# Attention with a leaky-ReLU network: chunk 3's x turned by the DMA crossbar, and product steps placed anew

## The chip, the core and the metric

The kernel runs on one core of a Trainium2 chip. A core has five engines with instruction streams of their own: TensorE (PE, matrix products into PSUM; its weight loads are listed as PEld), VectorE (DVE), ScalarE (ACT), GpSimd (POOL) and SyncE (SP). They meet only at semaphores. Here POOL's and SP's main work is to issue DMA transfers: POOL those that also convert fp32 to bf16, SP the others, among them the DMA transposes ("crossbar"). The metric is the device time of one execution in microseconds.

## What is computed

Attention over 4 batches, 8 heads, 768 positions and 64 values a head, and behind it a two-layer network on the result:

```python
scores = scale * np.matmul(q, k.transpose(0, 1, 3, 2))
causal = rel >= 0
stream_keep = causal & (is_sink | in_win)      # 4 sink keys, window of 64
mask = np.where(retr[0, :, 0, 0, None, None], full_mask, stream_mask)
scores = np.where(mask[None, :, :, :], scores, -1000000000.0)
a = np.exp(scores - max) / sum
x = (a @ v).transpose(0, 2, 1, 3).reshape(3072, 512)
h = x @ w_in                                   # 512 -> 2048, "product 1"
out = np.maximum(0.01 * h, h) @ w_out          # 2048 -> 512, "product 2"
```

Heads 0, 2 and 6 are "retrieval" heads (all earlier keys), the other five are "stream" heads (sinks and window).

## The kernel before

The 3072 rows are cut into eight chunks of 384 (`CH`). `ORDER` (L57) gives each chunk its batch and half: chunks 2 and 3 are the second halves of batches 0 and 1, chunks 4 and 5 the first halves of batches 2 and 3, chunks 6 and 7 their second halves.

The order of work is written out by hand as lists of closures. `run` calls them in order; since each engine's stream is in order, this sets the order on every engine. There are three kinds:

- *Slots* of attention (`Attention.slots`, L413). A second-half chunk has 21 units: five for each retrieval head (groups of keys), one for each stream head, and one for the sinks. In slot t, unit t gets its scores (TensorE into a `psS` bank, L329 for retrieval, L364 for stream, L309 for sinks), the exponential on ACT (L334, L369, L312), and a mask on DVE where one is needed (L337, L339, L373). In the same slot the unit `lag` slots earlier is multiplied with the values (L298, into a `po` bank). After the last unit of a pair of heads, `finish` (L386) adds the sinks' part, and DVE divides by the sums (`linv` L395, `xs` L397). Then x must be turned, so that the features lie along the partitions: `x_t` (L400).
- *Ticks* of product 1 (`in_slots`, L557): four matmuls of 128x384 (L563) into a `ph` bank and a leaky ReLU on ACT into `g` (L565); 16 in a chunk. Each tick reads the turned x (`xt`) of all four pairs of heads.
- *Steps* of product 2 (`out_slots`, L582): 2 to 4 matmuls of 128x512 (L589) into a `py` bank; after 5, 5 and 6 steps a tile of 128 rows is complete, DVE copies it (L595) and SP sends it out (L596); 16 steps in a chunk.

Each tag of PSUM has two banks (`BANKS`, L54): `ph`, `psS`, `po`, `py`.

`x_t` has two ways. Without `cross`, three transposes on TensorE (L407) go into a PSUM bank, and ACT (L409) or DVE (L411) copies it into `xt`; this happens three slots after `finish`, so that such an attention has 21 + `lag` + 3 slots. With `cross`, SP issues one DMA transpose from `xs` to `xt` (L402) right after `finish`, and there are 21 + `lag` slots.

Chunks 0 and 1 are done at the start. Then L783 runs chunk 2's attention (`lag` 3, transposes on TensorE into `ph`, copies on ACT; 27 slots) merged with 14 steps of product 2: the last four of chunk 0 and the first ten of chunk 1. `merge` (L618) spreads one list evenly over another. After it come stages n = 2 to 7 (loop at L787). Stage n does the ticks of chunk n, the steps of chunk n-1 and the attention of chunk n+1. `turn_dma(n+2)` puts two crossbar transfers of keys and queries on SP, `v_shift` two copies of values, `load_qk` and `load_v` further loads on POOL, and `spreads(n+2)` are DVE copies that spread the turned keys into `kt`; they are laid into slots (`both`, `into`). In stage 2, chunk 3's attention turns x on TensorE into `psS` banks with copies on DVE (27 slots). From stage 3 on (`n > 2`), attentions use the crossbar, and the last nine places of the list (`rest`) come after the attention, to cover the transfer.

Before the change, L798 to L807 set this:

```python
a = Attention(n + 1, xt_eng="v", cross=n > 2).slots(lag=2 if n > 2 else 3)
a = into(a, extra) if n > 2 else a
ms = merge(in_slots(n), outs)
rest = ms[-9:] if a and n > 2 else []
```

Of the kernel before, what the change touches and what calls it, by code (L numbers as in the profile page):

```python
# [21 lines left out]
def kernel(  # L22
# [36 lines left out]
    def bank(tag, shape, dtype):  # L59
        return ps.tile(shape, dtype, name=tag, tag=tag, bufs=BANKS[tag])  # L60
# [46 lines left out]
    def load_qk(n, nms="kq"):  # L107
        b, c = ORDER[n]
        for nm in nms:
            t = rot.tile([128, 3, H, D], BF16, name=f"{nm}b", tag=f"{nm}b", bufs=1)  # L110
            raw[nm, n] = t
            for g in range(3):
                nc.gpsimd.dma_start(out=t[:, g], in_=nat[nm][b, c, :, :, g])  # L113

    def load_v(n, gs=range(3)):
        b, c = ORDER[n]
        for g in gs:
            nc.gpsimd.dma_start(out=va[b][:, 3 * c + g, :, 0:D], in_=nat["v"][b, c, :, :, g])  # L118
# [3 lines left out]
    def load_sinks(b, eng=None):  # L122
        vsf[b] = rot.tile([32, D], FP32, name="vsf", tag="vsf", bufs=2)
        (eng or nc.sync).dma_start(out=vsf[b][:], in_=v[b, :, 0:NS, :])

    def sink_values(b, eng):
        n = H - 1
        eng.tensor_tensor(
            vs[b % 2][0:32, 1:H, 0:D],
            vsf[b].rearrange("p (o d) -> p o d", o=1).to_broadcast([32, n, D]),  # L130
            m_sink[0:32, 1:H].rearrange("p (h o) -> p h o", o=1).to_broadcast([32, n, D]),
            op=ALU.mult)
# [8 lines left out]
    def v_shift(n, eng=None):  # L141
        eng = eng or nc.sync
        i, c = ORDER[n]
        lo, hi = (0, 2) if c == 0 else (2, 5)
        eng.dma_start(out=vb[i][0:64, lo:hi], in_=va[i][64:128, lo:hi])
        eng.dma_start(out=vb[i][64:128, lo:hi], in_=va[i][0:64, lo + 1 : hi + 1])
# [77 lines left out]
    def turn_dma(n):  # L224
        qx[n] = rot.tile([128, 3, 4, 128], BF16, name="qd", tag="qd", bufs=3)
        raw["kx", n] = rot.tile([128, 3, 4, 128], BF16, name="kd", tag="kd", bufs=2)
        for nm, dst in (("k", raw["kx", n]), ("q", qx[n])):
            nc.sync.dma_start_transpose(out=dst.rearrange("p g q t -> p (g q) t"),
                                        in_=raw[nm, n].rearrange("p g h d -> p (g h d)"))

    def spreads(n):
        b, c = ORDER[n]

        def spread(g, hh):
            r = slice(64 * hh, 64 * hh + 64)
            o = CH * c + 128 * g
            nc.vector.tensor_copy(kt[b % 2][hh][r, :, o : o + 128], raw["kx", n][r, g])  # L237

        r = [lambda g=g, hh=hh: spread(g, hh) for g in range(3) for hh in range(2)]
        if c == 0:  # L240
            r += sink_keys_by(b)
        return r
# [4 lines left out]
    def into(slots, extra):  # L247
        r, extra = [], list(extra)
        for j, s in enumerate(slots):
            r.append(s)  # L250
            if 5 * j >= 2 * len(slots) and extra:
                r.append(extra.pop(0))
                if len(extra) > len(slots) - j - 2:
                    r.append(extra.pop(0))
        return r + extra
# [301 lines left out]
    def in_slots(n, tags=("ph",)):  # L557
        def tick(t):
            if n not in gs:
                gs[n] = rot.tile([128, NG, CH], BF16, name="g", tag="g", bufs=2)  # L560
            ph = bank(tags[t % len(tags)], [128, 512], FP32)
            for g in range(KG):
                nc.tensor.matmul(ph[:, 0:CH], lhsT=w_in_bf[:, g, 128 * t : 128 * t + 128],  # L563
                                 rhs=xts[n][:, g, :] if n else xts[0][:, :, g, :], start=(g == 0), stop=(g == KG - 1))
            nc.scalar.activation(out=gs[n][:, t, :], in_=ph[:, 0:CH], func=ACTF.Prelu, alpha=0.01)  # L565

        return [lambda t=t: tick(t) for t in range(NG)]
# [14 lines left out]
    def out_slots(n, tags=("py", "py", "py"), halves=False):  # L582
        slots = []

        def part(tt, lo, hi, tag, c0, c1):
            if lo == 0:
                py[n] = bank(tag, [128, 512], FP32)
            for ng in range(lo, hi):
                nc.tensor.matmul(py[n][:, 0 : c1 - c0], lhsT=gs[n][:, ng, 128 * tt : 128 * tt + 128],  # L589
                                 rhs=w_out_bf[:, ng, c0:c1], start=(ng == 0), stop=(ng == NG - 1))  # L590
            if hi == NG:
                o = rot.tile([128, DM], FP32, name="o", tag="o", bufs=6)
                b, c = ORDER[n]
                r0 = S * b + CH * c + 128 * tt
                nc.vector.tensor_copy(o[:, 0 : c1 - c0], py[n][:, 0 : c1 - c0])  # L595
                nc.sync.dma_start(out=out[r0 : r0 + 128, c0:c1], in_=o[:, 0 : c1 - c0])  # L596

        for tt in range(3):
            if halves and tt == 2:
                slots.append(lambda: part(2, 0, NG, "py", 0, 256))  # L600
                slots.append(lambda: part(2, 0, NG, "psS", 256, 384))
                slots.append(lambda: part(2, 0, NG, "po", 384, 512))
                continue
            lo = 0
            for w in ([3, 3, 3, 3, 4], [3, 3, 3, 3, 4], [3, 3, 3, 3, 2, 2])[tt]:
                slots.append(lambda tt=tt, lo=lo, w=w: part(tt, lo, lo + w, tags[tt], 0, DM))
                lo += w
        return slots

    def run(*lists):  # L610
        for l in lists:
            for f in l:
                f()

    def both(s, e):
        return lambda: (s(), e and e())

    def merge(ms, as_):  # L618

        r, done = [], 0  # L620
        for j, m in enumerate(ms):
            want = (j + 1) * len(as_) // len(ms)
            r += as_[done:want] + [m]
            done = want
        return r + as_[done:]
# [152 lines left out]
    o0, o1 = out_slots(0), out_slots(1)  # L778
# [1 line left out]
    run(spreads(2))  # L780
    run(o0[6:12])
    v_shift(3)
    run(merge(o0[12:] + o1[0:10], Attention(2, xt_tag="ph").slots(lag=3)))  # L783
    run(spreads(3))
    outs = o1[10:]

    for n in range(2, NCH):  # L787
        a, extra = [], ()
        if n + 2 < NCH:
            turn_dma(n + 2)  # L790
            v_shift(n + 2)
            extra = spreads(n + 2)
            if ORDER[n + 2][1] == 0:
                load_sinks(ORDER[n + 2][0], nc.gpsimd)
                sink_values(ORDER[n + 2][0], nc.gpsimd)
            if n + 3 < NCH:
                load_qk(n + 3)
                load_v(n + 3)  # L798
        if n + 1 < NCH:
            a = Attention(n + 1, xt_eng="v", cross=n > 2).slots(lag=2 if n > 2 else 3)  # L800
            a = into(a, extra) if n > 2 else a
        ms = merge(in_slots(n), outs)
        rest = ms[-9:] if a and n > 2 else []
        if n == 2:
            a, rest = [both(s, e) for s, e in zip(a[:-3], [None] * 16 + extra)], [ms[-4], a[-3], ms[-3], a[-2], a[-1], ms[-2], ms[-1]]
            ms = ms[:-4] + rest
        run(merge(ms[: len(ms) - len(rest)], a), rest)  # L807
        outs = out_slots(n) if n + 1 < NCH else out_slots(n, ("psS", "psS", "py"), True)
    run(outs)
# [35 lines left out]
```

## Time and profile before

| | us |
|---|---|
| median of five runs | 235.76 |
| lowest and highest | 234.3, 236.02 |
| the profiled execution | 235.92 |
| its span in the profile | 234.1 |

The runs are 235.92, 236.02, 234.3, 235.76 and 234.76 us. The profile is of one execution; its span runs from the first to the last instruction, so that the execution's time is 1.8 us longer. The profile lists each instruction with line, engine, start and duration. "L563 PE MATMUL ph<-xt,w_in_bf 128x384 x4" reads: four matmuls of line 563, which read `xt` and `w_in_bf` and write 384 columns of a `ph` bank. "[0.24 <-DVE xs L397]" means that the engine stood idle for 0.24 us before and that DVE's instruction of L397 ended this. The next stage boundaries can be read from the first score of each attention: chunk 2's at 56.05 us, chunk 3's at 72.96, chunk 4's at 95.73, chunk 5's at 120.54.

The sixteen crossbar transfers of x that are there before (chunks 4 to 7) take 1.18 us of SP's time each in the median, and 2.3 to 7.7 us from issue to landing, 5.0 in the median.

### The profile page before, as it was taken

How to read it: one execution, taken by the hardware profiler on the slowest of the kernel's cores; microseconds unless marked ns; L12 is line 12 of the kernel's file. 1: busy time of each engine (PE TensorE's matmuls, PEld its weight loads, DVE VectorE, ACT ScalarE, POOL GpSimd, SP SyncE). 2: the span in 40 equal slices, each digit the busy share in tenths (PEclk: the TensorE clock that was granted, in tenths of full speed). 3: DMA queues.
4: the chain of work that ended last, by engine and by line, in shares of the span. 5: the costliest groups of instructions: out<-in, count | busy, mean ns of one | idle time of the engine just before them, and what ended most of it. 6: DMA issues, size and time to landing. Idle time of an engine off the chain costs nothing.

```text
span 234.1 us, 5117 instructions
## 1 busy us (share of the span) xinstructions
PE 225.6 (96%) x2080; PEld 139.5 (60%) x2080; DVE 98.4 (42%) x282; ACT 127.9 (55%) x275; POOL 71.3 (30%) x87
## 2 busy tenths in 40 slices
PE   7868999999999999999999999999999999999995
PEld 5657876645664676666556655666556665555554
DVE  7885568014566357357324451156212341111122
ACT  5757765722775785655355545765556763434300
POOL 8949534207419319439104800000000000000000
PEclk9999999999999999999999999999999999999999
DMA  9999999999999999999999992920210221111112
GB/s 132 152 166 180 194 207 167 179 117 160 157 143 262 180 167 127 172 171 153 135 144 186 175 138 80 215 64 18 81 45 0 64 59 40 45 45 45 43 50 91
DMA packets 109481, 28.98 MB, mean 124 GB/s; under 512 B 101249, under 2 KB 105745, under 8 KB 109457
## 3 DMA queue, kind: packets, MB, share of 16 engines
q0 software_dynamic: 77088, 13.39, 78.2%
q1 hardware_dynamic: 31312, 15.00, 32.2%
q10 hardware_dynamic: 1056, 0.26, 0.5%
q8 instruction: 16, 0.26, 0.5%
q14 instruction: 9, 0.07, 0.1%
HBM read 27.30 MB, written 6.29 MB: 143 GB/s over the span
## 4 chain that ended last, share of the span: by engine, by line
PE 87%; POOL 5%; DMA 4%; DVE 1%; ACT 0%; issue 0%; POOLq 0%
PE py L589 31%; PE ph L563 30%; PE po L298 7%; PE psS L329 5%; DMA w_in_bf<-in_moe_w_in_dram 4%; PE psS L589 3%; PE psS L364 3%; PE psS L563 2%; PE psS L309 2%; PE ph L576 1%; POOL kb L113 1%; POOL va L118 1%; POOL qb L113 1%; POOL k L104 1%; POOL q L105 1%; DVE xs L397 1%
## 5 line engine op out<-in xcount | busy, mean ns | idle before, releaser
L589 PE MATMUL py<-w_out_bf,g 128*128 128x512 bf16 (+1 forms) x352 | 90.9, 374 | 0.0
L563 PE MATMUL ph<-xt,w_in_bf 128*128 128x384 bf16 x448 | 90.3, 326 | 0.0
L565 ACT ACTIVATE g<-ph 128x384 bf16<-128x384 f32 x112 | 55.0, 491 | 57.4 <-PE ph L563 56.4
L563 PEld LDWEIGHTS <-w_in_bf 128*128 128x128 bf16 x480 | 44.1, 98 | 31.3
L589 PEld LDWEIGHTS <-g 128*128 128x128 bf16 x416 | 35.9, 98 | 25.8
L334 ACT ACTIVATE at<-psS 128x384 bf16<-128x384 f32 x78 | 36.9, 488 | 18.6 <-PE psS L329 18.4
L595 DVE COPY o<-py 128x512 f32<-128x512 f32 (+1 forms) x22 | 14.9, 678 | 50.7 <-PE py L589 50.3
L113 POOL DMA_DIRECT2D kb<-in_k_dram x21 | 18.7, 904 | 32.6 <-DMA kd<-kb 31.9
L329 PE MATMUL psS<-qd,kt 128*128 128x384 bf16 (+2 forms) x90 | 23.0, 294 | 0.4 <-ACT at L334 0.3
L118 POOL DMA_DIRECT2D va<-in_v_dram x24 | 21.4, 911 | 5.1 <-DMA w_in_bf<-in_moe_w_in_dram 3.3
L113 POOL DMA_DIRECT2D qb<-in_q_dram x21 | 18.7, 910 | 5.9 <-DMA w_in_bf<-in_moe_w_in_dram 1.8
L298 PE MATMUL po<-va,at 128*128 128x65 bf16 x228 | 19.2, 193 | 0.0
L369 ACT ACTIVATE ats<-psS 128x384 bf16<-128x384 f32 x35 | 16.7, 488 | 3.6 <-PE psS L364 3.1
L373 DVE TENSOR_TENSOR ats<-ats,m_win 128x384 bf16<-128x384 bf16 x35 | 12.4, 358 | 14.0 <-ACT ats L369 13.4
L298 PEld LDWEIGHTS <-at 128*128 128x128 bf16 x234 | 14.8, 98 | 4.8 <-issue 0.2
L397 DVE TENSOR_TENSOR xs<-po,linv 128x384 bf16<-128x384 f32 x27 | 15.0, 557 | 0.9
L237 DVE COPY kt<-kd 64x512 bf16<-64x512 bf16 x36 | 14.5, 403 | 1.5 <-DMA kd<-kb 1.0
L329 PEld LDWEIGHTS <-kt 128*128 128x128 bf16 x99 | 9.4, 97 | 8.0 <-issue 0.9
L364 PEld LDWEIGHTS <-kt 128*128 128x128 bf16 x210 | 10.6, 98 | 5.4
L339 DVE TENSOR_TENSOR at<-at,m_caus 128x128 bf16<-128x128 bf16 x21 | 4.7, 223 | 21.4 <-ACT at L334 21.3
L298 PEld LDWEIGHTS <-ats 128*128 128x128 bf16 x210 | 10.4, 97 | 4.0 <-DVE xs L397 0.4
L395 DVE RECIPROCAL linv<-po 128x6 f32<-128x6 f32 x27 | 5.2, 193 | 15.7 <-PE po L298 15.7
(143 smaller groups left out, 206.6 us busy)
## 6 DMA issues: line engine op xcount, KB each, us to landing
out_dram<-o SPq DMA_DIRECT2D x23, 256.0 KB, 3.2
va<-in_v_dram POOLq DMA_DIRECT2D x24, 128.0 KB, 7.6
kb<-in_k_dram POOLq DMA_DIRECT2D x21, 128.0 KB, 5.3
qb<-in_q_dram POOLq DMA_DIRECT2D x21, 128.0 KB, 7.0
w_in_bf<-in_moe_w_in_dram POOLq DMA_DIRECT2D x4, 512.0 KB, 10.1
w_out_bf<-in_moe_w_out_dram POOLq DMA_DIRECT2D x4, 512.0 KB, 13.4
vb<-va SPq DMA_DIRECT2D x8, 195.0 KB, 4.1
vb<-va SPq DMA_DIRECT2D x4, 130.0 KB, 3.4
```

Of the source, the lines that this page charges most:

```text
L113: nc.gpsimd.dma_start(out=t[:, g], in_=nat[nm][b, c, :, :, g])
L118: nc.gpsimd.dma_start(out=va[b][:, 3 * c + g, :, 0:D], in_=nat["v"][b, c, :, :, g])
L298: nc.tensor.matmul(o, lhsT=lhsT, rhs=rhs, start=first, stop=False, skip_group_check=True)
L329: nc.tensor.matmul(s[:, off : off + w], lhsT=kt[i][hh][:, p, 128 * kj : 128 * kj + 128], rhs=q_of(n, p, lo, CH), start=(j == 0), stop=(j = ...
L334: nc.scalar.activation(out=a[:, 0:off], in_=s[:, 0:off], func=ACTF.Exp, scale=SM)
L364: nc.tensor.matmul(s[:, 64 * m : 64 * m + 64], lhsT=kt[i][hh][:, p, k0 : k0 + 128], rhs=q_of(n, p, 64 * m, 64 * m + 64), start=(m == 0), s ...
L369: nc.scalar.activation(out=av_, in_=s[:, 0:CH].rearrange("p (j e f) -> p j e f", j=3, e=2), func=ACTF.Exp, scale=SM)
L397: nc.vector.tensor_tensor(xs[:], po[:, :, :, 0:D], linv.to_broadcast([128, 3, 2, D]), op=ALU.mult)
L563: nc.tensor.matmul(ph[:, 0:CH], lhsT=w_in_bf[:, g, 128 * t : 128 * t + 128], rhs=xts[n][:, g, :] if n else xts[0][:, :, g, :], start=(g == ...
L565: nc.scalar.activation(out=gs[n][:, t, :], in_=ph[:, 0:CH], func=ACTF.Prelu, alpha=0.01)
L589: nc.tensor.matmul(py[n][:, 0 : c1 - c0], lhsT=gs[n][:, ng, 128 * tt : 128 * tt + 128], rhs=w_out_bf[:, ng, c0:c1], start=(ng == 0), stop= ...
L595: nc.vector.tensor_copy(o[:, 0 : c1 - c0], py[n][:, 0 : c1 - c0])
```

## The change

Three edits. First, all attentions from chunk 3 on use the crossbar (`cross=True`); chunk 3's has 24 slots instead of 27. Second, stage 3 begins with the first eight steps of chunk 2's product 2 (`outs[:8]`); the other eight are merged with its 16 ticks. Third, a new function `tail` lays four places of a list among the first three slots of another and puts the other slots behind them; it is used for the end of chunk 2's attention and of chunk 3's. For chunk 2's, ten steps are merged with the first 12 slots and the last four go through `tail` with the other 15 slots.

```diff
+    def tail(ms, a):
+
+        return [a[0], ms[0], a[1], ms[1], a[2], ms[2], ms[3], *a[3:]]
...
-    run(merge(o0[12:] + o1[0:10], Attention(2, xt_tag="ph").slots(lag=3)))
+    a2, m2 = Attention(2, xt_tag="ph").slots(lag=3), o0[12:] + o1[0:10]
+    run(merge(m2[:10], a2[:12]), tail(m2[10:], a2[12:]))
...
-            a = Attention(n + 1, xt_eng="v", cross=n > 2).slots(lag=2 if n > 2 else 3)
+            a = Attention(n + 1, cross=True).slots(lag=2 if n > 2 else 3)
             a = into(a, extra) if n > 2 else a
-        ms = merge(in_slots(n), outs)
+        ms = outs[:8] + merge(in_slots(n), outs[8:]) if n == 3 else merge(in_slots(n), outs)
         rest = ms[-9:] if a and n > 2 else []
         if n == 2:
-            a, rest = [both(s, e) for s, e in zip(a[:-3], [None] * 16 + extra)], [ms[-4], a[-3], ms[-3], a[-2], a[-1], ms[-2], ms[-1]]
-            ms = ms[:-4] + rest
+            a = [both(s, e) for s, e in zip(a, [None] * 15 + extra + [None])]
+            rest = tail(ms[-6:-2], a[-3:]) + ms[-2:]
+            ms, a = ms[:-6] + rest, a[:-3]
```

Counted from the order of instructions that this gives: chunk 2's attention from slot 15 to slot 26 has no product step between its slots (before, steps stood among them to the end). In stage 2 the eight spreading copies move from slots 16 to 23 to slots 15 to 22. In the stages from 4 on TensorE's order is as before. On SP, the four transfers of chunk 3's x stand behind chunk 4's value shifts and ahead of an output transfer and chunk 5's transposes.

## The prediction

> **What bounds the kernel now.** I read the page first, then the waits, then windows by stage, then the timeline of the two places that the change touches. Busy times and the chain of the page:
>
> ```profile
> PE 225.6 (96%) x2080; PEld 139.5 (60%) x2080; DVE 98.4 (42%) x282; ACT 127.9 (55%) x275; POOL 71.3 (30%) x87
> ...
> PE 87%; POOL 5%; DMA 4%; DVE 1%; ACT 0%; issue 0%; POOLq 0%
> ```
>
> TensorE carries 87% of the chain that ended last. So only three things count here: matmuls removed, new time in which TensorE stands still, and old time in which it stands still. A busy row says little about the last two, since matmuls overlap (a 128x384 one shows 0.33 us, yet four start 0.65 us apart): I compare starts. The windows of the two touched stages and the following one, and below them four early microseconds:
>
> ```profile
> 56.05:72.96 16.91, 16.67 (x194) 10.41 (x193) 7.56 (x21) 11.12 (x25) 8.63 (x10) 1.00 1.91 178
> 72.96:95.73 22.77, 22.42 (x235) 14.42 (x234) 13.69 (x39) 16.43 (x37) 13.94 (x17) 1.00 1.77 167
> 95.73:120.54 24.81, 24.81 (x212) 14.73 (x211) 11.36 (x30) 12.82 (x29) 9.52 (x12) 1.00 1.62 155
> ...
> 16.00:20.00 4.00, 2.19 (x35) 2.01 (x36) 2.61 (x10) 1.70 (x4) 2.30 (x3) 1.00 2.00 177
> ```
>
> The columns are length, then busy time of PE, PEld, DVE, ACT and POOL, then the granted clock. The end of chunk 2's attention:
>
> ```profile
> 70.87 0.81 PE L589 MATMUL py<-w_out_bf,g 128*128 128x512 bf16 x3
> 71.08 0.20 DVE L395 RECIPROCAL linv<-po 128x6 f32<-128x6 f32 x1 [1.02 <-PE po L298]
> 71.31 0.56 DVE L397 TENSOR_TENSOR xs<-po,linv 128x384 bf16<-128x384 f32 x1
> 71.92 0.34 PE L407 MATMUL ph<-ident,xs 128*128 128x128 bf16 x3 [0.24 <-DVE xs L397]
> 72.30 0.49 ACT L409 ACTIVATE xt<-ph 128x384 bf16<-128x384 bf16 x1 [2.25 <-PE ph L407]
> ```
>
> The three product steps from 70.87 keep TensorE supplied until 71.52; the transposes start at 71.92. So 0.40 us is lost, although the chain from weighted values to transposed x takes 1.05 us: a step of 0.65 us covers the rest, and the step after the transposes (0.86 us) covers their copy on ACT. In chunk 3's attention:
>
> ```profile
> 88.36 0.33 PE L407 MATMUL psS<-ident,xs 128*128 128x128 bf16 x3
> 89.01 0.33 PE L329 MATMUL psS<-qd,kt 128*128 128x256 bf16 x2 [0.32 <-ACT at L334]
> ```
>
> Three transposes take 0.16 us, so the score could start at 88.52; it starts at 89.01, because the transposes hold one of two psS banks and the other is still read by an exponential. Start to start I find 0.49 us lost here, 0.08 before the transposes at 82.87, and 0.14 and 0.21 near 74.6 and 75.8, where scores wait for exponentials and for DVE's spreading of keys.
>
> **The change, part by part.** Times are us.
>
> Part 1, chunk 3's x by crossbar: twelve transposes go, 4 x 0.16 = -0.65 on TensorE. The four DVE copies (0.35 each) go too, and are worth nothing: DVE is busy 13.69 of 22.77. With the transposes go their two waits, -0.49 and -0.08. The stage's first slots get a product step between third and fourth score, and DVE spreads the keys of chunk 3 before, while TensorE waits in part 2; that takes away up to the other 0.35. Sum -1.57; lower end of the gain 0.65 (waits reappear elsewhere).
>
> Part 2, the tail of chunk 2's attention. This attention has 27 slots, not 18. The new order puts the last four product steps after slots 12, 13 and 14 (the last two together), so that slots 15 to 26 run with none between: six score units, six weightings, three sets of transposes. Their work on TensorE by the timeline's spacings: five scores at 0.16, one stream unit 0.17, weightings 1.45 (three of 0.27, one of 0.19, five of 0.09), transposes 3 x 0.16: 2.90; with the next score (0.16) and first tick of product 1 (0.65) 3.71. What it takes, counted from the end of the last product step: score to exponential 0.36 (72.96 to 73.33), start of an exponential to the score that reuses its bank 0.54 (88.47 to 89.01), ACT's pitch 0.385 (pairs listed at 0.87). Scores at 0.00, 0.43, 0.90, 1.34; exponentials at 0.36, 0.80, 1.26, 1.70. DVE first empties the product's bank (0.20 to 0.81), then linv and xs of the second pair end at 1.60; the fourth pair's weightings use that pair's po bank, so they start at 1.65 and the transposes at 1.74, the fifth score at 1.90, the sixth (bank) at 2.24. ACT copies x at 2.12, exponentials 2.51 and 2.89. The last mask follows 0.52 behind (69.18 to 69.70) and takes 0.36: weightings 3.82, linv 4.30 (0.48, as 70.60 to 71.08), xs 4.53, transposes 5.14, copy 5.52 to 6.01. The first tick's fourth matmul reads that copy: 6.06, over at 6.22. Lost 6.22 - 3.71 = 2.51, against 0.40: +2.11.
> Bounds. Below: only the covering step of 0.65 is missing, +0.65. Above: the score slots are serial, 0.36 + 0.54 = 0.90 each, the sixth exponential at 4.86 and not 2.89, end 8.19: 4.48 lost, +4.08. I take 2.11: ACT's and DVE's rows give it instruction by instruction.
>
> Part 3, the next stage begins with eight steps of product 2 (chunk 2's, ready): same matmuls, another order, 0. It covers the crossbar. From the last weightings of chunk 3 to its first tick stand five ticks (3.25), two product steps and a part (0.43), then eight (5.4) and five slots: about 10. Needed: 1.3 from weightings to issue (113.59 to 114.86 for chunk 4) and 2.3 to 7.7 to landing, the spread of the sixteen such transfers; chunk 5's first tick at 120.71 shows no wait 5.9 after issue. Queues: SP now issues four transposes of about 1.2 behind chunk 4's value shifts and ahead of the out transfer and chunk 5's key transposes. It stands idle from 87.6 to 95.4, so three lie there; the last adds about 1.2 ahead of an out transfer that waits for its copy anyway. POOL's loads of chunk 6 come behind chunk 5's transposes; no row of TensorE after 96 waits for a load. Price 0; if that cover is gone, the first tick of chunk 3 waits.
> ACT sees fewer evacuations while the eight steps run and denser ones later: a tick is 0.65 and its evacuation 0.49; old stage three had ACT busy 12.82 of 24.81. Price 0, bounds 0 and 0.5.
>
> The clock: the window 16 to 20 has TensorE busy 2.19 of 4.00, with one idle stretch of 1.26, at granted clock 1.00. My tail's longest idle stretch is 1.05 (4.09 to 5.14). I add nothing.
> The Trainium skill, "TensorE: Matmul & The Clock Gate", section "HAM oscillation", warns against idle gaps over about 3.4 us, after which the clock halves; were that to strike here, an estimate is one such window at half speed, +1.7, a sum of 238.0. The rule speaks against gathering idle time in a tail, but this gap stays under it.
>
> Sum: +2.11 - 1.57 = +0.54 on an execution of 235.92 (span 234.1 and 1.8 around it): 236.5. The median of the runs is 235.76, 0.16 lower, so the forecast for it is 236.3.
>
> **The rivals.** First, serial score slots: in the tail each score waits for the exponential just before, as at 89.01, because ACT is late with copies. Place: slots 15 to 20; price +4.08 - 1.57 = +2.5, 238.3, slower. For it: that row. Against: two psS banks alternate and ACT's pitch is 0.385. It decides from a tail of 6.9 (a loss of 2.75) upward.
> Second, the tail costs little: weightings fill the gaps and only the missing step shows, +0.65 - 1.57 = -0.9, 234.8. For it: the six score slots hold 2.3 of work against 2.7 of chain. Against: the finishing chain of 1.05 has nothing beside it.
> Third, the crossbar isn't in time: the last transfer has to share the queues with a pair of key and query transposes (up to 6.4 of issue), landing 15.4 after the weightings where 10 are covered: +5.4, 241.7 with the sum. Against: those stand behind it on SP.
>
> **How the numbers follow.** Forecast 0.54, serial slots 0.29, cheap tail 0.13, late crossbar 0.04. A measurement of this kernel can tell about 0.5%, 1.2 us. No change by that: 0.50 of the forecast's 0.54 and 0.06 of the cheap tail's 0.13. Slower: serial slots 0.29, late crossbar 0.04, 0.03 of the forecast. Faster: the cheap tail's other 0.07, where some gain that I don't see is added, and 0.01 of the forecast. Range: from the cheap tail, 234.9, to the serial slots, 238.3; outside lie the late crossbar, the worst of both bounds at once (+4.08 - 0.65, 239.2) and parts of both edges.
>
> **What would show it.** The stretch from chunk 2's first score to chunk 3's first: 16.91 now, 18.9 forecast (16.91 - 0.40 + 2.41). From there to chunk 4's first score: 22.77 becomes about 21.3. The tail's weightings should wait for DVE, one transpose row should show some 1.05 idle. No L407 or L411 rows after 80, four more transposes at L402. No wait for a DMA at the first tick of chunk 3. Wrong would be a tail over 6.9, a wait for xt at L563, a clock under 1.00, or waits in stage three.

## The result

The changed kernel takes 235.55 us in the median of 43 runs (234.56 to 237.97), the kernel before 234.81 in the median of 80 run beside it: a ratio of 1.004, 95% interval 1.0026 to 1.0054. It is slower by 0.4%, which is inside the half per cent that the prediction called no change (the interval ends just above it), and on the side where its sum lay (+0.54 us forecast; the ratio stands for +0.6 to +1.3 us). Here and below, a ratio leaves out executions that took over 1.5% more than the fastest of the same kernel.

The page of one changed execution (span 233.1 us, its time 234.84):

```profile
PE 224.2 (96%) x2068; PEld 138.7 (60%) x2068; DVE 98.2 (42%) x278; ACT 128.5 (55%) x275; POOL 71.2 (31%) x87
...
PE 88%; POOL 4%; DMA 3%; ACT 2%; DVE 2%; issue 0%; POOLq 0%
```

Twelve matmuls and four DVE copies are gone; TensorE still carries the chain. This span is a microsecond shorter than the one shown of before, which is no gain: chunk 1's sink scores, ahead of anything that the change touches, start at 25.56 us here and at 27.31 there, and over all profiles of this study that start lies between 25.1 and 28.0. So I compare stretches. The windows from chunk 2's first score to chunk 3's, on to chunk 4's and on to chunk 5's (columns as in the prediction):

```profile
54.30:73.08 18.78, 17.30 (x195) 10.64 (x194) 8.27 (x24) 10.94 (x24) 11.19 (x14) 1.00 1.69 210
73.08:94.41 21.33, 21.33 (x225) 13.76 (x223) 13.02 (x33) 16.72 (x38) 11.53 (x14) 1.00 2.01 157
94.41:119.22 24.81, 24.81 (x212) 14.73 (x211) 10.63 (x30) 13.31 (x29) 8.89 (x10) 1.00 1.40 151
```

The first stretch grew from 16.91 to 18.78 (+1.87), the second shrank from 22.77 to 21.33 (-1.44), the third is the same to the hundredth. Net +0.43. The tail of chunk 2's attention in the timeline, from its first bare score to the first tick of product 1, all engines, a selection:

```profile
67.70 0.33 PE L329 MATMUL psS<-qd,kt 128*128 128x384 bf16 x1
...
68.14 0.33 PE L329 MATMUL psS<-qd,kt 128*128 128x384 bf16 x1
...
68.61 0.32 PE L329 MATMUL psS<-qd,kt 128*128 128x384 bf16 x1
...
69.12 0.33 PE L329 MATMUL psS<-qd,kt 128*128 128x384 bf16 x1
...
70.02 0.34 PE L364 MATMUL psS<-qd,kt 128*128 128x64 bf16 x6
...
70.61 0.51 ACT L369 ACTIVATE ats<-psS 128x384 bf16<-128x384 f32 x1
70.77 0.29 DVE L337 TENSOR_TENSOR at<-at,m_caus 128x256 bf16<-128x256 bf16 x1 [0.53 <-ACT at L334]
...
71.12 0.27 PE L298 MATMUL po<-va,at 128*128 128x65 bf16 x3 [0.41 <-DVE at L337]
71.15 0.36 DVE L373 TENSOR_TENSOR ats<-ats,m_win 128x384 bf16<-128x384 bf16 x1
...
71.57 0.20 PE L298 MATMUL po<-vb,ats 128*128 128x65 bf16 x1 [0.18 <-DVE ats L373]
...
72.06 0.20 DVE L395 RECIPROCAL linv<-po 128x6 f32<-128x6 f32 x1 [0.55 <-PE po L298]
72.29 0.56 DVE L397 TENSOR_TENSOR xs<-po,linv 128x384 bf16<-128x384 f32 x1
...
72.90 0.34 PE L407 MATMUL ph<-ident,xs 128*128 128x128 bf16 x3 [0.88 <-DVE xs L397]
73.08 0.33 PE L329 MATMUL psS<-qd,kt 128*128 128x384 bf16 x1
...
73.24 0.90 PE L563 MATMUL ph<-xt,w_in_bf 128*128 128x384 bf16 x4
73.28 0.49 ACT L409 ACTIVATE xt<-ph 128x384 bf16<-128x384 bf16 x1 [1.77 <-PE ph L407]
```

Read it from the bracket at the end of the lines from 70.77 on: TensorE waits for a mask, for the next mask, then for the division, while nothing else is queued. The first tick's four matmuls take 0.90 instead of 0.81, since the fourth waits for the copy that ends at 73.77. In the second stretch, the place where a score used to wait for a psS bank now reads:

```profile
87.77 0.33 PE L329 MATMUL psS<-qd,kt 128*128 128x384 bf16 x1
87.93 0.25 PE L298 MATMUL po<-va,at 128*128 128x65 bf16 x3
88.02 0.81 PE L563 MATMUL ph<-xt,w_in_bf 128*128 128x384 bf16 x4
88.67 0.33 PE L329 MATMUL psS<-qd,kt 128*128 128x256 bf16 x2
```

Each starts when the one before has gone through (0.16, 0.09, 0.65): no transposes, no wait. The crossbar transfers are twenty now instead of sixteen, and nobody waits for them:

```profile
L402 SPq DMA_TRANSPOSE xt<-xs x20: 1179/1182/2252, 83.5 to 193.6; - x20
...
DMA to landing us min/median/max: 2.3/3.3/6.0
```

One thing doesn't show in this profile. In 11 of 44 executions of the changed kernel the mean granted clock is 0.991 to 0.993, else 0.998 to 1.000. Those 11 take 237.09 us in the mean, the other 33 take 235.36. I call such an execution one with a dip. Of another 80 executions of the kernel before, measured beside the experiments, 4 have a dip; the other 76 take 234.87 in the mean. So at full clock the change costs 235.36 - 234.87 = +0.49 us (standard error 0.14), as in the stretches; executions with a dip, a quarter of all and 1.7 us longer in the mean, add about 0.4 to the mean, where 4 of 80 add about 0.1 to that of the kernel before. Chance alone would seldom give 11 of 44 against 4 of 80 (0.003 by Fisher's exact test).

### The profile page after: what moved, and what is told of

It reads as the page before. It is cut to its first block, busy times and chain, and to the rows that moved or that the text cites. A ratio compares the mean times of both kernels' runs of the same rounds, so it can differ in the third digit from the quotient of the medians.

```text
span 233.1 us, 5099 instructions
## 1 busy us (share of the span) xinstructions
PE 224.2 (96%) x2068; PEld 138.7 (60%) x2068; DVE 98.2 (42%) x278; ACT 128.5 (55%) x275; POOL 71.2 (31%) x87
## 4 chain that ended last, share of the span: by engine, by line
PE 88%; POOL 4%; DMA 3%; ACT 2%; DVE 2%; issue 0%; POOLq 0%
PE py L589 32%; PE ph L563 30%; PE po L298 6%; PE psS L329 5%; PE psS L589 3%; DMA kb<-in_k_dram 3%; PE psS L364 3%; PE psS L563 2%; PE ph L576 2%; PE psS L309 2%; ACT at L334 1%; POOL va L118 1%; POOL k L104 1%; POOL q L105 1%; DVE xs L397 1%; POOL kb L113 1%
## 5 line engine op out<-in xcount | busy, mean ns | idle before, releaser
L329 PE MATMUL psS<-qd,kt 128*128 128x384 bf16 (+2 forms) x90 | 23.1, 294 | 0.0
L237 DVE COPY kt<-kd 64x512 bf16<-64x512 bf16 x36 | 15.1, 419 | 0.6
L339 DVE TENSOR_TENSOR at<-at,m_caus 128x128 bf16<-128x128 bf16 x21 | 5.4, 260 | 20.7 <-ACT at L334 20.6
```

The source lines that it names most:

```text
L329: nc.tensor.matmul(s[:, off : off + w], lhsT=kt[i][hh][:, p, 128 * kj : 128 * kj + 128], rhs=q_of(n, p, lo, CH), start=(j == 0), stop=(j = ...
```

## The experiments

Each run was compared with the kernel before on the same chip. "Stretch" is the time in one profile from chunk 2's first score to chunk 4's: 39.68 before, 40.11 after. "Dips" counts the executions with a mean clock of 0.993 or below.

**Even end: the crossbar and the new head of stage 3 without the tail.**

```diff
-    run(merge(m2[:10], a2[:12]), tail(m2[10:], a2[12:]))
+    run(merge(m2, a2))
```

> The changed kernel with chunk 2's attention merged evenly with its 14 product steps again, as before the change; the crossbar for chunk 3 and the eight product steps at the head of stage 3 stay. If the sum of the prediction holds (tail +2.1, crossbar and freed banks -1.57), this is 1.57 us faster than the kernel before: 0.9933 of it; the stretch from chunk 2's first score to chunk 3's is 16.9 and from there to chunk 4's 21.3. If the loss of the change lies in the crossbar part or the new head of stage 3 instead, it is no faster than before. If dips of the granted clock come from the tail, its runs show 0.991 to 0.993 about as seldom as the kernel before.

Measured: ratio 0.9986 (0.996 to 1.0013); stretch 16.91 + 21.35 = 38.26, so -1.42, close to the forecast -1.57; no dip in 12 executions. The stretch confirms the second part of the sum. The ratio does not show all of it.

**The tail alone, on the kernel before.**

```diff
-    run(merge(o0[12:] + o1[0:10], Attention(2, xt_tag="ph").slots(lag=3)))
+    a2, m2 = Attention(2, xt_tag="ph").slots(lag=3), o0[12:] + o1[0:10]
+    run(merge(m2[:10], a2[:12]), tail(m2[10:], a2[12:]))
```

> The kernel before with the new end of chunk 2's attention alone. By the sum: +2.1 us in executions at full clock, 1.009 of before, with the first stretch at 19.0 and the second at 22.4 to 22.8. If the clock's dips come from this tail, about a quarter of its runs show a mean granted clock of 0.991 to 0.993 and are 1.5 to 2 us longer still. If the tail is cheap (rival two): +0.65, 1.003.

Measured: ratio 1.0072 (1.0044 to 1.01), +1.7 us (+1.5 at full clock, in the mean of nine); stretch 18.78 + 22.65 = 41.43, +1.75; 2 dips in 11. The profile also has a wait of 0.47 us for the queries ahead of chunk 2's first score, outside the stretch. The two parts add up: +1.75 - 1.42 = +0.33 against +0.43 for the whole change. The cheap tail (+0.65) is excluded.

**No cover: crossbar for chunk 3, even end, but stage 3 begins as before.**

```diff
-        ms = outs[:8] + merge(in_slots(n), outs[8:]) if n == 3 else merge(in_slots(n), outs)
+        ms = merge(in_slots(n), outs)
```

> As the first, but stage 3 begins with ticks and steps in turn, as before the change: crossbar for chunk 3 with nothing put ahead to cover it. From the last weightings of chunk 3 some 3.2 us of work stand before its first tick, where the last transfer needs 1.3 to its issue and 2.3 to 7.7 to land. If the eight steps are what covers it: TensorE waits 0.4 to 5.8 at the first tick, some 3 in the middle, so the kernel is about 3 us slower than the first of these. If the transfer is quick enough anyway, the two are equal.

Measured: ratio 1.0142 (1.0104 to 1.0179), median 238.75; 4 dips in 6. The two executions at full clock take 237.25 in the mean, 2.8 more than the even end's 234.46, where some 3 were expected. Its timeline at chunk 3's first tick:

```profile
93.06 0.33 PE L329 MATMUL psS<-qd,kt 128*128 128x384 bf16 x1
93.22 0.33 PE L563 MATMUL ph<-xt,w_in_bf 128*128 128x384 bf16 x1
94.38 0.32 PE L563 MATMUL ph<-xt,w_in_bf 128*128 128x384 bf16 x1 [0.83 <-DMA xt<-xs]
96.49 0.47 PE L563 MATMUL ph<-xt,w_in_bf 128*128 128x384 bf16 x1 [1.79 <-DMA xt<-xs]
97.84 0.48 PE L563 MATMUL ph<-xt,w_in_bf 128*128 128x384 bf16 x1 [0.88 <-DMA xt<-xs]
```

The tick's four matmuls read the four pairs of heads, and each of the last three waits for its own transfer: 4.6 us from the first to the last instead of 0.5. The eight steps are what covers this. The windows of the same kernel, with the clock as third last column:

```profile
95.00:98.00 3.00, 0.63 (x2) 0.21 (x2) 0.00 (x0) 0.00 (x0) 0.00 (x0) 0.75 1.84 193
98.00:101.00 3.00, 3.00 (x18) 1.63 (x17) 0.49 (x2) 1.36 (x3) 0.00 (x0) 0.50 1.88 167
```

From 96.5 to 103.4 us, by the trace's clock record, TensorE runs at half clock, and most of this lies behind the wait: the wait is paid for a second time.

**Filled gaps: the changed kernel with matmuls of zeros where TensorE stands still.**

```diff
+    fill = {13: 5, 14: 3, 15: 9}
...
+        return lambda: (s(), idle("py", fill[j]) if j in fill else None)
```

> The changed kernel with 17 matmuls of zeros (128x256, 0.107 each, 1.8 us in all) put into the three longest gaps of the tail (0.53, 0.32 and 0.96 us), where TensorE stands still anyway. They compute nothing that is used. If the dips of the clock come from TensorE's low share of busy time there, the runs with 0.991 to 0.993 go, and the slow edge of its times with them, while the fast edge stays (within 0.2 us of the changed kernel's 234.6). If the dips have another cause, a quarter of the runs keep them.

Measured: 1.0049 (1.0018 to 1.0079); 3 dips in 12; the nine executions at full clock take 235.43 in the mean, as the changed kernel, and the stretch is 18.78 + 21.33, the same to the hundredth. The fill costs nothing, which says that the tail is bound by its chain. In the profile TensorE is busy without a break from 69.16 to 74.54. The dips did not go; by the expectation this speaks for another cause than the tail's idle time, but 12 executions are few.

**The even end once more.** The same kernel as the first.

> The kernel with chunk 2's attention merged evenly, once more, for a second profile and more executions. In its first profile the stretch from chunk 1's sink scores to the last copy of the output took 202.6 against 204.0 before, so by that it is 1.4 us faster (0.994); the first comparison gave 0.9986 [0.996, 1.0013]. If the difference is the time at which the loads at the start let chunk 1 begin (it was 25.6 to 27.3 us in six profiles), the stretches after that are the same in this profile, whatever its total, and the ratio comes nearer to 0.994. If the kernel now waits for transfers in some executions, a wait of TensorE for a DMA shows after 50 us.

Measured: 0.9957 (0.9921 to 0.9993); 3 dips in 12, so with its first 12 executions this kernel without a bare tail has 3 in 24. From chunk 1's sink scores to chunk 7's it takes 149.3 us, against 149.0 in its first profile, 150.4 before and 150.85 after the change. So the gain of 1.1 to 1.4 us is there in both profiles.

**Covered: three product steps between the last weightings and the last transposes.**

```diff
-    run(merge(m2[:10], a2[:12]), tail(m2[10:], a2[12:]))
+    run(merge(m2[:11], a2[:24]), m2[11:13], a2[24:], m2[13:])
```

> The changed kernel with chunk 2's product steps spread over slots 0 to 23, and three of them between the last weightings and the last transposes, the fourth behind these: nothing is left bare. By the sum the 0.40 us that the kernel before loses at the transposes go as well: 1.42 + 0.40 = 1.8 us faster than before, 0.992, and no dips of the clock. If the tail's loss is not the missing product steps, it is no better than the changed kernel, 1.004.

Measured: 0.9993 (0.9959 to 1.0027); 1 dip in 12. In its profile the stretch is 17.15 + 21.67 = 38.82, 0.86 less than before and not the 1.8 that I expected. The first part, where the 0.40 at the transposes was to be gained, is 0.24 longer than before. In the second a new wait took part of the gain:

```profile
76.60 0.27 PE L329 MATMUL psS<-qd,kt 128*128 128x256 bf16 x1
77.12 0.23 PE L329 MATMUL psS<-qd,kt 128*128 128x128 bf16 x1 [0.25 <-DVE kt L237]
```

DVE spreads chunk 3's keys after chunk 2's last division; when TensorE no longer stands still before that, it arrives first. This profile also shows a dip far from any tail, at the start of the program, in the windows:

```profile
16.00:20.00 4.00, 2.17 (x31) 1.73 (x29) 2.31 (x8) 1.61 (x4) 2.62 (x4) 0.96 2.02 177
20.00:24.00 4.00, 4.00 (x41) 3.73 (x40) 1.75 (x6) 2.46 (x5) 2.61 (x4) 0.61 1.96 175
```

**A longer bare tail: all 14 steps among the first 12 slots.**

```diff
-    run(merge(m2[:10], a2[:12]), tail(m2[10:], a2[12:]))
+    run(merge(m2, a2[:12]), a2[12:])
```

> All 14 product steps among the first 12 slots, so that 15 slots stand bare instead of 12; the longest gap, before the last transposes, stays about 1.05. The three more slots hold stream units and weightings, so TensorE loses some 0.5 to 1 us more: 1.007 to 1.009 of before at full clock. If the clock dips by the share of idle time in a stretch of 3.4 us, dips become more frequent (over half of the runs). If it dips by the length of one gap, they stay at a quarter or fewer.

Measured: 1.0081 (1.0049 to 1.0113); 4 dips in 12. Three more bare slots lengthen the way from chunk 1's sinks to chunk 7's by 0.7 us against the changed kernel. The dips, a third, tell neither way.

**Filled with data.** As the filled kernel, reading weights of product 1 in place of zeros.

```diff
-        return lambda: (s(), idle("py", fill[j]) if j in fill else None)
+        return lambda: (s(), busy(fill[j]) if j in fill else None)
```

> As the filled kernel, but the 17 matmuls in the gaps read weights of product 1 instead of zeros; the results are not used. Filled with zeros, three of twelve runs still showed 0.991 to 0.993. If matmuls of zeros don't count as activity for the clock, the dips go now; if the dips stay at a quarter, the gaps that were filled aren't their cause, and the half-busy stretch of small weightings before them, or something else, is.

Measured: 1.0033 (0.9999 to 1.0068); 1 dip in 12. Both fills together have 4 in 24, between the bare tail's quarter and the few per cent of before; so few runs tell neither apart.

**Keys earlier: the covered version with the spreading laid into chunk 2's slots.**

```diff
+    a2 = [both(s, e) for s, e in zip(a2, [None] * 17 + spreads(3) + [None] * 4)]
```

> The covered version with DVE's spreading of chunk 3's keys laid into slots 17 to 22 of chunk 2's attention, instead of behind it. In the covered version's profile the second score group of slot 4 of chunk 3 waits 0.35 us for that spreading. If this is what the covered version lost, the wait goes: the stretch from chunk 1's sink scores to chunk 7's becomes about 149.1 (covered 149.55, before 150.42), and the time 0.993 to 0.996 of before. If DVE's extra copies in the slots delay masks or divisions there, the same amount comes back before chunk 3's first score and nothing is gained.

Measured: 0.9998 (0.9963 to 1.0032), without the three executions that dip, which all took over 1.5% more than the fastest; 3 dips in 12, with no bare tail. The wait for the keys is gone from its profile, but other short ones stand there (0.2 for a mask, 0.2 for an exponential), and the way from sinks to sinks is 149.5, as in the covered version: nothing gained.

**A wider gap: three DVE copies ahead of the last division.**

```diff
+        for _ in range(3):
+            nc.vector.tensor_copy(o[:].rearrange(...), ident.rearrange(...).to_broadcast([128, 4, 128]))
...
+    run(merge(m2[:10], a2[:12]), tail(m2[10:], a2[12:23] + [dve_busy] + a2[23:]))
```

> The changed kernel with three copies more on DVE (128x512 into an unused buffer) just before the last division of chunk 2, so that the last gap of the tail grows by 1 us or somewhat more, from 1.05 to about 2; the copies' results are not used. If the clock's dips come from the idle time that the tail gathers in one stretch of 3.4 us, more than half of the runs now show 0.991 to 0.993 (a quarter before), and a profile in such a run shows the half clock begin within 3.4 us of the tail's end. If the dips come from elsewhere, they stay at a quarter and the kernel is about 1 us slower than the changed one in all runs.

Measured: 1.0146 (1.0102 to 1.0191); 4 dips in 6, one of them to 0.984. The gap grew more than planned, to 2.73 us (0.88 by the same bracket in the changed kernel). The profile fell on an execution with a dip; its timeline and windows:

```profile
74.26 0.34 PE L407 MATMUL ph<-ident,xs 128*128 128x128 bf16 x3 [2.73 <-DVE xs L397]
...
75.63 0.53 PE L329 MATMUL psS<-qd,kt 128*128 128x384 bf16 x1
75.95 1.49 PE L563 MATMUL ph<-xt,w_in_bf 128*128 128x384 bf16 x4
```

```profile
71.42:74.84 3.42, 0.69 (x10) 0.46 (x7) 3.27 (x7) 0.20 (x1) 3.29 (x5) 1.00 1.70 253
74.84:78.25 3.41, 3.41 (x12) 1.54 (x11) 1.15 (x4) 2.31 (x6) 0.00 (x0) 0.50 2.26 176
```

A single 128x384 row grows from 0.33 to 0.53, and four take 1.49 instead of 0.81: half clock, by the trace's record from 74.84 to 78.25 us, 3.41 long, just behind the tail. So idle time gathered in a tail can bring a dip, here with TensorE busy 0.69 of the 3.42 us ahead of it. The way from chunk 1's sinks to chunk 7's is 154.24, 3.4 longer than in the changed kernel; the wider gap is 1.85 of this, which leaves an estimate of 1.5 for the half clock. The tail of the changed kernel is less idle, and this run does not show that it does the same.

**The even end in two single executions.** The same kernel as the first, for a profile of a long execution.

> The kernel with the even end again, for a profile of a longer execution: without dips of the clock its 21 executions spread from 232.9 to 235.9, the 61 of the kernel before from 233.7 to 236.2. If an execution of 235 or more owes its length to the start, chunk 1's sink scores stand at 27 us or later and the stretch from there to chunk 7's is 148.9 to 149.4 as in the two profiles. If TensorE, which now runs ahead, meets late transfers in some executions, the stretch is longer by 1 us or more, with a wait for a DMA or for DVE's spreading in it.

> The same as the look before it, since one execution alone may fall among the short ones: a start at 27 us or later with a stretch of 148.9 to 149.4, or a stretch longer by 1 us or more.

Measured: 233.67 and 233.3 us, the kernel before 235.13 beside them; both fell among the short executions, with 149.4 us from chunk 1's sinks to chunk 7's. The spread that the expectation names leaves out the longest of the 21, 237.46 us. In the second profile TensorE waits 0.31 us for a crossbar transfer at chunk 4's first tick (118.34 us).

## Why the prediction held, point by point

**The tail** was worked out at 6.22 us from the end of the last product step to the end of the first tick. Measured: 67.70 to 73.98 (73.24 plus the tick's 0.65 and the 0.09 that its last matmul waits), 6.28. The last weightings began at 71.57, 3.87 after the step's end (3.82 forecast); transposes at 5.20 (5.14), first tick at 5.54. What the chain hung on was named correctly: not the exponentials, whose pace nearly fits the work beside them, but the last masks and the division. Its price was somewhat high. Alone on the kernel before it adds 1.87 to the first stretch and 0.09 to the first tick, 1.96 against the forecast +2.11; in the same run 0.21 comes back, because DVE's spreading is ready when chunk 3's scores need it, which the prediction had booked with the crossbar. Together that is the +1.75 of the stretch.

**Crossbar and freed banks** were put at -1.57. The even end shows -1.42, with -1.44 in the changed kernel's second stretch. Transposes and bank wait are gone as described. The warning that the start's 0.35 hung on TensorE standing still before it came true: the covered version waits there for DVE, and so do two of the even end's four profiles (0.2 and 0.3 us).

**The cover for the crossbar** was priced at nothing, with a wait at the first tick if it is gone. With it, no wait at chunk 3's first tick in any profile; without it, 4.1 us more at that tick.

**Stage 3's new order** cost nothing: 24.81 both times.

**The level** was off, and did no harm by luck. The 236.3 stands on the median of five executions, 235.76, where the later 80 give 234.81; the result of 235.55 still lies in the range of 234.9 to 238.3.

**The clock** is the step that failed. The prediction added nothing for it, and named a clock under 1.00 as a sign of being wrong; 11 of 44 executions show it. "I add nothing" rested on one window, 16 to 20 us, in one execution, where TensorE was half idle at a granted clock of 1.00. The covered version's profile has the same window, as idle (busy 2.17 of 4.00), with the clock at half right behind it (19.7 to 23.1 us). So one trace can't exclude a dip. An execution with a dip takes 1.7 us more in the mean, which is the size that the prediction's sentence on the rule had estimated, though part of this can be a late start, as in the covered version's profile. Weighted by a quarter, the sum would have been +0.54 + 0.4, about +0.9, which is the middle of the measured interval.
The Trainium skill ("TensorE: Matmul & The Clock Gate", section "What's actually happening") says that the clock is decided by activity in a free-running window of 3.4 us. The traces agree: the half-clock stretches inside the program are 3.41, 3.41 and 6.83 us long, and the times between changes of the clock are whole multiples of 3.413 us in every trace that has some, counted from a first change that lies between 3.9 and 6.6 us and differs from execution to execution. Cut into such windows, the thirteen traces that record changes hold 862 at full clock. In nine of them TensorE is busy 46% of the time or less, and half clock follows each of the nine, three inside the program and six at its end. In the other 853 it is busy 51% or more, and none is followed by half clock. The highest of the nine (covered), the lowest of the others (before), and one that lies on the bare tail (the tail alone; busy time of PE after the comma):

```profile
16.30:19.71 3.41, 1.58 (x23) 1.18 (x21) 1.98 (x7) 1.14 (x3) 2.04 (x4) 1.00 2.03 176
...
15.45:18.86 3.41, 1.73 (x31) 1.37 (x26) 2.44 (x10) 1.14 (x2) 1.16 (x2) 1.00 2.27 161
...
70.98:74.39 3.41, 1.94 (x34) 1.44 (x33) 2.16 (x9) 1.64 (x5) 3.41 (x5) 1.00 1.34 268
```

The Trainium skill's rule of thumb on the same page, no idle gaps over about 3.4 us (section "HAM oscillation"), was too generous: half clock came behind windows whose longest gaps were 2.73 us (wider gap), 1.79 us (no cover) and 0.88 us (covered).
Whether the changed kernel's dips come from its tail is not shown. The bare tails dip in 17 of 67 executions (changed, tail alone, longer tail), but the versions with an even or covered end do so in 7 of 50, and so few do not tell the two apart. No profile fell on a dip of a bare tail. In two profiles, the tail alone and the longer tail, a window lies almost where the tail is most idle, with TensorE busy 1.94 and 1.93 of 3.41 us, and the clock stays full. The one dip seen without a widened or uncovered wait lies at the start of the program, where TensorE waits for loads in the kernel before too. So the cause of the more frequent dips stays open.

**The rivals.** Serial score slots are excluded: scores at 67.70, 68.14, 68.61 and 69.12 stand 0.44 to 0.51 apart, where serial ones would stand 0.90 apart. The cheap tail is excluded by the tail alone. The late crossbar happened at chunk 3's first tick only where its cover was taken away. The first rival's threshold holds a slip: a tail of 6.9 is a loss of 3.19 by the prediction's own 3.71 of work, not 2.75; the measured 6.28 lies below it either way.

**What stays open.** At full clock the even end takes 234.11 in the mean of 22 executions, 0.8 (error 0.2) below the kernel before, where its four profiles give 1.0 to 1.4; the covered version shows no gain in the mean where its profile gives 0.9. The profiles say where most of the spread lies: in all fourteen, the execution's time is the start of chunk 1's sinks, the way from there to chunk 7's, and 58.2 to 58.6 us more. The covered version's 235.94 is a start at 27.97 and a way of 149.55, and the 233.05 with the keys earlier a start at 25.14 and a way of 149.47: the start, ahead of anything that was changed, makes the difference. No profile fell on a long execution of the even end, so whether these are of the same kind was not seen.

## What to carry to other kernels

When filler work is taken from a chain of dependent steps, count the slots that are left bare and follow the chain to its end: here the last masks, division, transposes and copy, 3 us without a product step beside them, cost more than the transposes that the change saved. Where filler steps stand matters less than that some stand there: three of them put behind the last weightings (covered) gained no more than steps spread evenly. Idle time on TensorE can cost twice, since half clock may follow it in a share of the executions; look at the granted clock of many executions, not of one profile.

The best version found keeps the crossbar and the eight leading steps and drops the tail: 0.9986 and 0.9957 of before in two comparisons, the second clear of 1 by its interval (0.9921 to 0.9993), the first not.

## What the hardware showed beside that

The crossbar lands four transfers of one attention one after the other: without cover the first tick's last three matmuls started 1.2, 3.3 and 4.6 us after the first, each released by its own transfer. And a fill of 17 matmuls in the tail's gaps left the time at full clock unchanged (235.43 and 235.59 against 235.36), so such fills were free here, though their effect on the clock could not be settled with 24 executions.
